# Sums and differences of x on Pool, and S1 as 64x64 TensorE tiles between S2 and S3

## The chip, the cores and the metric

The kernel runs on one core of one Trainium2 chip. The metric is the device time of one execution in microseconds (us), as the median of the fast runs. The engines are named as the profile names them: PE is TensorE's matmul and PEld its weight load, DVE is VectorE, ACT is ScalarE, POOL is GpSimd, SP is SyncE, which here only issues transfers. L377 is line 377 of that version of the kernel; the lines move a little from version to version. The code and diffs below are shortened; ... marks a cut inside a line or between lines.

Ratios below are the mean time of one kernel's runs over that of the other's runs of the same rounds on the same chip, so they are not quite the ratios of the medians that are quoted beside them.

## The reference

```python
X = np.fft.rfft(x, axis=1)                     # x: 8 x 3072 x 256, fp32
y = np.fft.irfft(X * (filt_r + 1j*filt_i), n=3072, axis=1)
t = y.reshape(24576, 256)
g = np.maximum(t @ w1, t @ w2)                 # w1, w2: 256 x 1024
out = g @ w_out                                # 1024 x 256
```

A long convolution by way of the Fourier transform is followed by a two-way maximum network on each of the 24,576 tokens.

## The kernel before

The transform of length 3072 = 128 x 24 is done with matmuls in four stages. S1 is a real transform of length 128 (table `C1`) for each of 24 columns. S2 is the 24-long transform with its twiddles (`U`), in 32 groups `t`. The filter is a multiplication on DVE. S3 goes back (`VP`, `VQ`), and S4 is the last transform of length 128 (`G1`). Between S1 and S2, and between S3 and S4, the data makes a round trip through HBM (`ad` to `bt`, `zd` to `zr`), which transposes it. The network is computed as relu(y(w1 - w2)) w_out + y(w2 w_out): `ph` is the first matmul, `gt` its relu, `po` the sum of both parts, `ot` the output tile of 512 tokens.

Batch 0 is done in a startup of about 49 us. From there on each tile of 512 tokens is 8 "steps". A step is one `ph` pair and one half of a `po`, about 1 us. A plan in the program hangs the transform's pieces for later batches onto step numbers. The program fixes the order of every engine's instructions.

```python
xpool = tile_pool(name="xpool", bufs=8)
apool = tile_pool(name="apool", bufs=5)          # at
pqpool = tile_pool(name="pqpool", bufs=6)
...
ps = tile_pool(name="ps", bufs=6, space=PSUM)    # px, pa, pz, ph, py share six banks
pso = tile_pool(name="pso", bufs=2, space=PSUM)  # po
opool = tile_pool(name="opool", bufs=2)          # ot: two output buffers

def load_x(b, c):                                # Pool issues it; fp32 becomes bf16 on the way
    t_ = xpool.tile([128, 4, D], BF16)
    G.dma_start(out=t_, in_=x[b].rearrange("(p n) d -> p n d", n=24)[:, 4*c:4*c+4, :])

def f1(b, c, E=None):                            # S1: one 128x128 matmul, 512 columns
    pa = ps.tile([128, 2, D], FP32)
    TE.matmul(pa, C1, xb[b, c // 2][:, 2*(c % 2):2*(c % 2)+2])
    evac(E or S, at[:, ...], pa)                 # ACT copies, SP writes at to HBM
    if c % 2 == 1: nc.sync.dma_start(out=ad[b][...], in_=at)

def f1_read(b):                                  # four transfers, SP
    bt[b] = bpool.tile([128, 32, D], BF16); ...

def gen_f2(b):                                   # eight groups per batch
    for g in (4, 5, 6, 7, 2, 3, 1, 0):
        px = two banks; eight matmuls px <- bt, U           # S2, 64x64 tiles
        pq = DVE: px * F                                    # two of 1.2 us
        S3 of the group before: pz = two banks; 16 matmuls; ACT copies pz to zt; SP writes zt
        yield

def moe_o(tt, j):                                # second half of the network
    ...
    if j % 4 == 3: V.tensor_copy(ot[tt][...], po[tt])       # DVE
    if j == 7:     G.dma_start(out=..., in_=ot[tt])         # Pool issues the output transfer

plan_x(n, ...)  -> load_x at given steps;  plan_f1(n, ...) -> f1 x 12, then f1_read
plan_f2(n, ...) -> nine calls of the group generator, then z_read
```

Of the kernel before, what the change touches and what calls it, by code (L numbers as in the profile page):

```python
# [8 lines left out]
FP32 = mybir.dt.float32  # L9
BF16 = mybir.dt.bfloat16  # L10
AF = mybir.ActivationFunctionType
OP = mybir.AluOpType

B = 8
# [15 lines left out]
def kernel(  # L30
# [38 lines left out]
    I128 = const.tile([128, 128], BF16)  # L69

    dram = ctx.enter_context(tc.tile_pool(name="dram", bufs=2, space=bass.MemoryType.DRAM))
    xpool = ctx.enter_context(tc.tile_pool(name="xpool", bufs=8))
    apool = ctx.enter_context(tc.tile_pool(name="apool", bufs=5))
    bpool = ctx.enter_context(tc.tile_pool(name="bpool", bufs=2))
    pqpool = ctx.enter_context(tc.tile_pool(name="pqpool", bufs=6))
    zpool = ctx.enter_context(tc.tile_pool(name="zpool", bufs=2))
    zrpool = ctx.enter_context(tc.tile_pool(name="zrpool", bufs=2))
    late = ctx.enter_context(tc.tile_pool(name="late", bufs=1))
    w2b = late.tile([128, 2, HID], BF16)
    w2T = late.tile([128, 8, D], BF16)  # L80
    setup = ExitStack()
    ps = None
    init = setup.enter_context(tc.tile_pool(name="init", bufs=1))
# [4 lines left out]
    def bank2(shape, dtype, name, tag=None):  # L88
        if tag is None:
            ring.append(ring.pop(0))  # L90
            tag = ring[-1]
        return p2.tile(shape, dtype, tag=tag, name=name)
# [63 lines left out]
    def patch_f0():  # L156
        nc.sync.dma_start(out=F0[12:13, 1, 0], in_=filt_i[1536:1537, :])
        nc.sync.dma_start(out=F0[12:13, 0, 0], in_=filt_r[1536:1537, :])
# [45 lines left out]
    load_f(1)  # L204

    Ct = init.tile([128, 128], BF16)

    def table_c():
        V.memset(kc[:, :, 1, 0:1], 32.0)
        V.memset(kc[:, 1, 0, 0:1], 64.0)  # L210
        p128 = init.tile([128, 1], FP32)
        V.tensor_scalar(p128, pid, 1.0 / 128.0, None, OP.mult)
        uc = init.tile([128, 2, 2, T], FP32)
        rc = init.tile([128, 2, 2, T], FP32)
        V.tensor_scalar(uc[:, 0], kc[:, 0], p128, 0.25, OP.mult, OP.add)
        V.tensor_scalar(uc[:, 1], kc[:, 1], p128, 0.5, OP.mult, OP.add)
        V.tensor_scalar(uc[:, 1, 0, 0:1], kc[:, 1, 0, 0:1], p128, 0.25, OP.mult, OP.add)
        V.tensor_scalar(rc, uc, RND, RND, OP.add, OP.subtract)
        V.tensor_tensor(uc, uc, rc, OP.subtract)
        for a in range(2):  # L220
            for b in range(2):
                S.activation(Ct.rearrange("p (b a h c u) -> p a b c h u", b=2, a=2, h=4, c=2)[:, a, b],
                             uc[:, a, b].rearrange("p (c h u) -> p c h u", c=2, h=4), AF.Sin, bias=zero, scale=TWO_PI)
        Cv = C1.rearrange("p (h c u b a) -> p a b c h u", h=4, c=2, b=2, a=2)
        for a in range(2):
            for b in range(2):
                S.activation(Cv[:, a, b], uc[:, a, b].rearrange("p (c h u) -> p c h u", c=2, h=4),
                             AF.Sin, bias=zero, scale=TWO_PI)
# [56 lines left out]
    def table_e(t1):  # L285
        V.tensor_scalar(t1, pid, 12.0, None, OP.is_equal)
        V.tensor_scalar(e0[:, 0:1], pid, 0.0, t1, OP.is_equal, OP.add)
        V.tensor_scalar(e0[:, 1:2], e0[:, 0:1], -1.0, 1.0, OP.mult, OP.add)
        V.tensor_scalar(e0[:, 0:1], e0[:, 0:1], -0.5, 1.0, OP.mult, OP.add)
        V.memset(F0[:, :, :, 0:1], 0.0)  # L290

    def sines_u(q):
        Uv = U.rearrange("p t (r x) -> p t r x", r=2)
# [13 lines left out]
        G.tensor_copy(F[0:64, :, 1, 0], F0[:, :, 1])  # L307

    def tables_pe():
        pv = bank2([128, 16, 2, 64], BF16, "pv")  # L310
        for u in range(16):
            TE.transpose(pv[:, u], U[:, 2 * u:2 * u + 2].rearrange("p c x -> p (c x)"), I128)
        V.tensor_copy(VP[:, :, :, 0:48], pv[:, :, :, 0:48])

    def table_g():
        pg = p2.tile([128, 128], BF16, tag="px", name="pg", bufs=4)
        TE.transpose(pg, C1, I128)
        S.activation(G1, pg, AF.Copy)

    def tables_q(h, E):  # L320
# [49 lines left out]
    def f1(b, c, E=None):  # L370
# [8 lines left out]
        if c % 2 == 1:  # L379
            nc.sync.dma_start(out=ad[b][:, 2 * c - 2:2 * c + 2], in_=at)  # L380

    def f1_read(b):
        bt[b] = bpool.tile([128, T, D], BF16, tag="bt", name="bt")
        src = ad[b].rearrange("(t b a) n d -> b (a n) t d", b=2, a=2)
        for h in (1, 0):
            for blk in range(2):
                nc.sync.dma_start(out=bt[b][64 * blk:64 * blk + 48, 16 * h:16 * h + 16],  # L387
                                  in_=src[blk][:, 16 * h:16 * h + 16])


    def z_read(b, h):
# [5 lines left out]
    def gen_f2(b):  # L397
        bt_ = bt[b]
        zd[b] = dram.tile([T, 96, D], BF16, tag="zd", name="zd")
        pend = []  # L400
        zt = None

        def s3(g, pq):
            nonlocal zt
            if zt is None:
                zt = zpool.tile([128, 2, 4, D], BF16, tag="zt", name="zt")
                made.clear()
            pz = [ps.tile([128, 2, D], FP32, tag="ps", name="pz") for _ in range(2)]
            for i in range(2):
                for ri, W in enumerate((VP, VQ)):  # L410
                    for c, k in QUADS:
                        TE.matmul(pz[c][64 * k:64 * k + 64, i], W[64 * c:64 * c + 56, 2 * g + i, k],  # L412
                                  pq[k][64 * c:64 * c + 56, ri, i], start=(ri == 0), stop=(ri == 1))
            o = 2 * (g % 2)
            for c in range(2):
                S.activation(zt[0:ROWS, c, o:o + 2], pz[c][0:ROWS], AF.Copy)  # L416
            made.append(g)
            if len(made) == 2:
                t0 = 8 * (g // 2)
                for k in range(2):  # L420
                    nc.sync.dma_start(out=zd[b][t0:t0 + 8, 48 * k:48 * k + 48].rearrange("t p d -> p t d"),
                                      in_=zt[64 * k:64 * k + 48].rearrange("p c u d -> p (c u) d"))
                zt = None

        made = []
        for g in (4, 5, 6, 7, 2, 3, 1, 0):
            px = [ps.tile([128, 2, D], FP32, tag="ps", name="px") for _ in range(2)]
            for i in range(2):
                for k, c in QUADS:
                    t_ = 8 * (g // 2) + 4 * c + 2 * (g % 2) + i  # L430
                    TE.matmul(px[k][64 * c:64 * c + 64, i], U[64 * k:64 * k + 48, 4 * g + 2 * i + c],  # L431
                              bt_[64 * k:64 * k + 48, t_], start=True, stop=True)
            pq = []
            for k in range(2):
                pq.append(pqpool.tile([128, 2, 2, D], BF16, tag="pq", name="pq"))
                V.tensor_tensor(pq[k][0:FROWS],  # L436
                                px[k][0:FROWS].rearrange("p (o i) d -> p o i d", o=1).to_broadcast([FROWS, 2, 2, D]),
                                F[0:FROWS, :, k, 2 * g:2 * g + 2], OP.mult)
            pend.append((g, pq))
            if len(pend) > 1:  # L440
                s3(*pend.pop(0))
            yield
        while pend:
            s3(*pend.pop(0))
        yield
# [152 lines left out]
            pass  # L598

    table_c()  # L600
    Zt = late.tile([128, 2, 128, N2], BF16, name="Zt")
    At = init.tile([128, 4, 64, T], BF16, name="At")
    zeros(At[:, :, 48:64].rearrange("p h m t -> p h (m t)"), [4, 512])
    zeros(U.rearrange("p t (q x) -> p (t q) x", q=2)[:, :, 24:32], [64, 8])
# [17 lines left out]
    sines_u(1)  # L622
    first_s1(2, S)
    expand_f(5, 0, V)
    sines_u(2)
    first_s1(3, S)
    expand_f(0, 0, V)
    first_s1(4, V, 2)
    first_s1(5, S, 2)
    expand_f(6, 0, V)  # L630
    expand_f(1, 1, S, 2)
    table_e(t1)
    load_f0()
    patch_f0()
    first_t1(1, V)
    first_t1(2, V)
    expand_f(7, 0, S)
    pend = []
    for n, g in enumerate(order):
        pend.append(first_s2(g, n in (0, 1, 2, 4, 6)))  # L640
# [40 lines left out]
    def plan(step, fn, *a):  # L681
        todo.setdefault(step, []).append((fn, a))

    def plan_x(n, steps):
        for c, s_ in enumerate(steps):
            plan(s_, load_x, n, c)

    def plan_f1(n, steps, read):
        for c, s_ in enumerate(steps):
            plan(s_, f1, n, c)  # L690
        plan(read, f1_read, n)

    def plan_f2(n, steps, z1, z0):
        g = []
# [11 lines left out]
    def spaced(first, gap, count):  # L706
        return [first + int(gap * i) for i in range(count)]
# [4 lines left out]
        plan(int(0.6 * (c - 1)), f1, 1, c, (S, V)[c % 2])  # L712
    plan(6, f1_read, 1)
    plan_f2(1, spaced(17, 1.9, 9), 28, 34)
    plan_x(2, spaced(8, 4, 6))
    plan_f1(2, spaced(34, 1, 12), 46)
    plan_f2(2, spaced(60, 2.5, 9), 74, 81)
    plan_x(3, spaced(44, 4, 6))
    plan_f1(3, spaced(70, 1.5, 12), 88)
    plan_f2(3, spaced(104, 3, 9), 121, 129)  # L720
    plan_x(4, spaced(90, 4, 6))
    plan_f1(4, spaced(112, 1.8, 12), 132)
    plan_f2(4, spaced(151, 3.3, 9), 169, 179)
    for n in range(5, B):
        o = 48 * (n - 5)
        plan_x(n, spaced(138 + o, 4, 6))
        plan_f1(n, spaced(158 + o, 1.9, 12), 180 + o)
        plan_f2(n, spaced(197 + o, 3.4, 9), 216 + o, 226 + o)

    def in_f2(step):  # L730
# [44 lines left out]
```

## Time and profile before

| | before |
|---|---|
| time, median of 2 runs | 532.39 us (532.07 to 532.71) |
| profiled span | 529.9 us |
| TensorE's mean granted clock | 0.998 |

The first fence holds lines of the profile's page. The first line is the busy time of each engine. The next lines cut the span into 40 slices: the busy share of PE and of Pool in tenths, the clock granted to TensorE, and the busy share of the 16 DMA engines.

```profile
PE 509.2 (96%) x5133; PEld 346.6 (65%) x5212; DVE 321.9 (61%) x436; ACT 336.0 (63%) x597; POOL 77.5 (15%) x130
...
PE   8898999999999999999999999999999999999994
...
POOL 6684011111001200011001200021000000000000
PEclk9999999999999999999999999999999999999999
DMA  7993687877678947599468956699377826521122
```

After the first tenth PE is busy nearly always, at full clock. Pool is nearly idle. The DMA engines are not: several slices are at 9.

The timeline shows how long an S1 matmul and a group hold PE (columns: start, duration, engine, line, operation, output and inputs, shapes, count).

```profile
250.69 0.38 PE L377 MATMUL pa<-xb,C 128*128 128x512 bf16 x1
...
250.91 0.59 PE L558 MATMUL ph<-y__4122,Wd 128*128 128x512 bf16 x2
...
251.98 0.41 PE L431 MATMUL px<-bt,U 48*64 48x256 bf16 x8
...
252.22 0.28 PE L412 MATMUL pz<-pq,VP 56*64 56x256 bf16 x4
...
252.22 0.12 PEld L412 LDWEIGHTS <-VQ 56*64 56x64 bf16 x4
252.33 0.28 PE L412 MATMUL pz<-pq,VQ 56*64 56x256 bf16 x4
```

A matmul's duration includes its way through the pipeline, so the time that it holds PE is read from the next start: 0.22 us from pa to ph. Eight px tiles take 0.24 us and four pz tiles 0.11 us. A 128x128 matmul of 512 columns takes 0.22 us, so 256 columns take half of that, and these are the times of four tiles running side by side.

The list of waits (who waited for whom; total us, times, longest) shows how little slack there is on PE.

```profile
PE ph L558 <- DVE pq L436: 2.3, 7, 0.3
...
PE pz L412 <- DVE pq L436: 0.8, 1, 0.8
...
DVE ot L585 <- DMA out_dram<-ot: 2.7, 1, 2.7
```

In the groups of Pool's instructions there is one operation like the new fold:

```profile
L339 POOL TENSOR_TENSOR Wd<-wf 128x1024 bf16<-128x1024 f32 x2 | 4.7, 2358 | 0.0
```

The page's DMA part gives the two queues that matter: packets, MB, and the share of 16 engines' span. q1 carries what SP issues, q0 what Pool issues. The last line is the x transfer before the change: its count, its size, and the median time from issue to landing in us.

```profile
q1 hardware_dynamic: 52196, 44.84, 37.2%
q0 software_dynamic: 16208, 41.95, 30.6%
...
xb<-in_x_dram POOLq DMA_DIRECT2D x48, 256.0 KB, 8.1
```

### The profile page before, as it was taken

How to read it: one execution, taken by the hardware profiler on the slowest of the kernel's cores; microseconds unless marked ns; L12 is line 12 of the kernel's file. 1: busy time of each engine (PE TensorE's matmuls, PEld its weight loads, DVE VectorE, ACT ScalarE, POOL GpSimd, SP SyncE). 2: the span in 40 equal slices, each digit the busy share in tenths (PEclk: the TensorE clock that was granted, in tenths of full speed). 3: DMA queues.
4: the chain of work that ended last, by engine and by line, in shares of the span. 5: the costliest groups of instructions: out<-in, count | busy, mean ns of one | idle time of the engine just before them, and what ended most of it. 6: DMA issues, size and time to landing. Idle time of an engine off the chain costs nothing.

```text
span 529.9 us, 12176 instructions
## 1 busy us (share of the span) xinstructions
PE 509.2 (96%) x5133; PEld 346.6 (65%) x5212; DVE 321.9 (61%) x436; ACT 336.0 (63%) x597; POOL 77.5 (15%) x130
## 2 busy tenths in 40 slices
PE   8898999999999999999999999999999999999994
PEld 3556656666667666676667666676667666677774
DVE  8886579245854576348763677438763688443431
ACT  6786657856785588746775577655775566555540
POOL 6684011111001200011001200021000000000000
PEclk9999999999999999999999999999999999999999
DMA  7993687877678947599468956699377826521122
GB/s 145 285 189 62 162 167 174 228 215 170 170 207 222 218 132 213 144 197 208 143 212 164 261 134 175 186 191 224 112 203 207 146 94 160 130 80 79 42 81 79
DMA packets 68459, 87.57 MB, mean 165 GB/s; under 512 B 4082, under 2 KB 48756, under 8 KB 67412
## 3 DMA queue, kind: packets, MB, share of 16 engines
q1 hardware_dynamic: 52196, 44.84, 37.2%
q0 software_dynamic: 16208, 41.95, 30.6%
q8 instruction: 40, 0.66, 0.5%
q14 instruction: 15, 0.12, 0.1%
HBM read 54.79 MB, written 47.19 MB: 192 GB/s over the span
## 4 chain that ended last, share of the span: by engine, by line
PE 72%; DMA 3%; DVE 1%; issue 1%; ACT 0%; SPq 0%
PE po L583 28%; PE ph L558 24%; PE po L578 7%; PE pz L412 4%; PE px L431 3%; PE py L542 3%; PE pa L377 3%; DMA bt<-ad 2%; DVE pq L436 1%; DMA ad<-at 1%; DVE ot L585 0%; ACT y__5598 L545 0%; SPq L387 0%
## 5 line engine op out<-in xcount | busy, mean ns | idle before, releaser
L563 ACT ACTIVATE gt<-ph 128x512 bf16<-128x512 f32 x308 | 182.3, 599 | 109.4 <-PE ph L558 108.2
L583 PE MATMUL po<-Wo,gt 128*128 128x256 bf16 x1536 | 229.8, 273 | 3.0
L583 PEld LDWEIGHTS <-gt 128*128 128x128 bf16 x1536 | 150.3, 98 | 57.5
L436 DVE TENSOR_TENSOR pq<-px,F 120x1024 bf16<-120x1024 f32 x112 | 131.7, 1218 | 28.0 <-PE px L431 27.5
L585 DVE COPY ot<-po 128x512 f32<-128x512 f32 x96 | 66.2, 689 | 111.2 <-PE po L583 108.2
L558 PEld LDWEIGHTS <-Wd 128*128 128x128 bf16 x768 | 70.1, 98 | 27.8 <-issue 12.5
L590 POOL DMA_DIRECT2D out_dram<-ot x47 | 25.2, 537 | 430.8 <-DVE ot L585 409.5
L416 ACT ACTIVATE zt<-pz 112x512 bf16<-112x512 f32 x112 | 60.7, 594 | 43.1 <-PE pz L412 37.9
L561 DVE TENSOR_SCALAR gt<-ph 128x512 bf16<-128x512 f32 x76 | 52.1, 686 | 29.6 <-PE ph L558 22.5
L476 ACT ACTIVATE at<-pa 128x512 bf16<-128x512 f32 x78 | 46.8, 600 | 12.4 <-PE pa L377 10.7
L377 PE MATMUL pa<-xb,C 128*128 128x512 bf16 x83 | 31.1, 381 | 0.1
L542 PE MATMUL py<-G,zr 128*128 128x128 bf16 x384 | 29.4, 219 | 0.7 <-ACT zr L476 0.7
L412 PE MATMUL pz<-pq,VP 56*64 56x256 bf16 x448 | 28.5, 271 | 0.8 <-DVE pq L436 0.8
L412 PE MATMUL pz<-pq,VQ 56*64 56x256 bf16 x448 | 27.9, 268 | 0.0
L542 PEld LDWEIGHTS <-zr 128*128 128x128 bf16 x384 | 24.8, 98 | 3.7 <-issue 1.9
L101 POOL DMA_DIRECT2D xb<-in_x_dram x48 | 26.2, 556 | 1.5 <-DMA Fs<-in_filt_i_dram 1.3
L431 PE MATMUL px<-bt,U 48*64 48x256 bf16 x448 | 23.4, 281 | 0.1
L431 PEld LDWEIGHTS <-U 48*64 48x64 bf16 x448 | 8.2, 104 | 12.1 <-issue 11.8
L492 DVE TENSOR_TENSOR pq<-px,F 120x1024 bf16<-120x1024 f32 x11 | 13.2, 1221 | 3.8 <-PE px L483 1.3
L412 PEld LDWEIGHTS <-VP 56*64 56x64 bf16 x448 | 13.1, 106 | 2.7 <-issue 1.5
L476 ACT ACTIVATE F<-pf 128x1024 bf16<-128x1024 f32 x10 | 10.3, 1026 | 6.2 <-PE pf L134 5.8
L412 PEld LDWEIGHTS <-VQ 56*64 56x64 bf16 x448 | 13.2, 107 | 0.0
(383 smaller groups left out, 580.4 us busy)
## 6 DMA issues: line engine op xcount, KB each, us to landing
out_dram<-ot POOLq DMA_DIRECT2D x47, 512.0 KB, 4.5
xb<-in_x_dram POOLq DMA_DIRECT2D x48, 256.0 KB, 8.1
ad<-at SPq DMA_DIRECT2D x42, 256.0 KB
bt<-ad SPq DMA_DIRECT2D x28, 384.0 KB
zd<-zt SPq DMA_DIRECT2D x56, 192.0 KB
zr<-zd SPq DMA_DIRECT2D x14, 768.0 KB
wf<-in_moe_w_dram POOLq DMA_DIRECT2D x2, 1024.0 KB, 9.8
Fs<-in_filt_r_dram POOLq DMA_DIRECT2D x1, 768.0 KB, 7.0
```

The costliest lines, as they stand in the source:

```text
L377: TE.matmul(pa, C1, xb[b, c // 2][:, 2 * (c % 2):2 * (c % 2) + 2], start=True, stop=True)
L412: TE.matmul(pz[c][64 * k:64 * k + 64, i], W[64 * c:64 * c + 56, 2 * g + i, k], pq[k][64 * c:64 * c + 56, ri, i], start=(ri == 0), stop=(ri ...
L416: S.activation(zt[0:ROWS, c, o:o + 2], pz[c][0:ROWS], AF.Copy)
L431: TE.matmul(px[k][64 * c:64 * c + 64, i], U[64 * k:64 * k + 48, 4 * g + 2 * i + c], bt_[64 * k:64 * k + 48, t_], start=True, stop=True)
L436: V.tensor_tensor(pq[k][0:FROWS], px[k][0:FROWS].rearrange("p (o i) d -> p o i d", o=1).to_broadcast([FROWS, 2, 2, D]), F[0:FROWS, :, k, 2 ...
L476: S.activation(out_, in_, AF.Copy)
L542: TE.matmul(py[:, n], zr[b][:, 4 * i + n, 128 * dc:128 * dc + 128], G1, start=True, stop=True)
L558: TE.matmul(ph, Wd[:, dc, 128 * j:128 * j + 128], y_[:, dc].rearrange("p a b -> p (a b)"), start=(dc == 0), stop=(dc == 1))
L561: V.tensor_scalar(gt[tt][:, j], ph, 0.0, None, OP.max)
L563: S.activation(gt[tt][:, j], ph, AF.Relu)
L583: TE.matmul(p_, g_[:, jj, 128 * n:128 * n + 128], Wo[:, jj], start=False, stop=(jj == 7))
L585: V.tensor_copy(ot[tt][:, n - 1:n + 1], po[tt])
```

## The change

A transform of length 128 splits into two of half the contraction: even frequencies need x[p] + x[p+64], odd ones x[p] - x[p+64]. So for batches 2 to 7 x is loaded as fp32 with both rows side by side, Pool forms sum and difference in bf16, and S1 becomes four 64x64 tiles of 512 columns in place of two 128x128 matmuls. The four can run side by side, so S1 should take half of PE's time. S2 and S3 are 64x64 tiles already, so the S1 tiles of the next batch are put inside the groups, between px and pz, and need no change of tile mode.

```diff
+    def load_p(b, c):                     # SP issues it, fp32 stays fp32
+        if c == 0: big[b] = late.tile([128, 3, 2, 2 * D], FP32, tag="l0", name="xf")
+        xb[b, c] = big[b][:, c] if c < 3 else late.tile([128, 2, 2 * D], FP32, tag="l%d" % (c - 2))
+        for m in range(2):
+            nc.sync.dma_start(out=xb[b, c][64 * m:64 * m + 64], in_=...)
+    def fold_x(b, c):                     # Pool
+        xf = xb[b, c]
+        xb[b, c] = xpool.tile([128, 2, 2 * D], BF16, tag="xb", name="xd")
+        for i, op in enumerate((OP.add, OP.subtract)):
+            G.tensor_tensor(xb[b, c][:, i], xf[:, 0], xf[:, 1], op)
+    def f1_half(b, c):
+        ...
+        at = apool.tile([128, 4, D], BF16, tag="at", name="at")
+        pa = [ps.tile([128, 2, D], FP32, tag="ps", name="pa") for _ in range(2)]
+        for m, i in QUADS:
+            TE.matmul(pa[m][64*i:64*i+64], C1[64*m:64*m+64, 64*i:64*i+64], xb[b, c][64*m:64*m+64, i], ...)
+        for m in range(2): S.activation(at[:, 2*m:2*m+2], pa[m], AF.Copy)
+        nc.sync.dma_start(out=ad[b][:, 4*c:4*c+4], in_=at)
     # f1_read: eight transfers in place of four
     # gen_f2, in each group, after pq and before S3 of the group before:
+            if b + 1 < B and j in (0, 1, 3, 4, 6, 7):
+                f1_half(b + 1, (0, 1, 3, 4, 6, 7).index(j))
     def plan_x(n, steps):
         for c, s_ in enumerate(steps):
-            plan(s_, load_x, n, c)
+            plan(s_, load_p, n, c)
+            plan(s_ + 5, fold_x, n, c)
-    plan_f1(3, spaced(70, 1.5, 12), 88)
+    plan(83, f1_read, 3)
-    plan_x(4, spaced(90, 4, 6))
+    plan_x(4, spaced(76, 3.5, 6))
     ... (the other batches alike; small moves in the startup; xpool 8 -> 7 buffers; tables reordered)
```

## The prediction

> **What bounds the kernel now.** TensorE. The page gives PE 96% of the 529.9 us span, DVE 61%, ACT 63%, POOL 15%. The table by stretches shows PE busy 19.5 to 19.9 of every 20 us from 120 to 500 us at full clock. The list of waits holds only about 3.6 us in which PE sat before ph or pz. From the first ph matmul (49 us) on, a microsecond added to or taken from PE's in-order queue is a microsecond of time.
>
> **What the change removes.** In the timeline an S1 matmul (pa, 128x128, 512 columns) holds PE 0.22 us (250.69, next start 250.91). Twelve per batch, six batches: 15.5 us. Folding halves contraction and outputs, so six groups of four 64x64 matmuls replace twelve. The S2/S3 tiles show that four run together: eight px matmuls of 256 columns take 0.24 us, four pz 0.11 us. (The Trainium skill, "TensorEngine Tiling (Array Packing)", Key Properties, says so; this trace agrees.) So 36 x 0.22 = 7.9 us should leave PE. No mode switch is added: the tiles stand between S2 and S3 of the same mode.
>
> **What it adds off PE.** 72 Pool folds, estimated at 1.2 us each from Pool's 128x1024 subtraction (2.36 us): 85 us, on an engine 85% idle. x arrives as fp32 from the SP queue, some 20 steps before use. F1 reads are twice the issues, same bytes. I expect these hidden.
>
> **What it moves, and the catch.** Six PSUM banks serve px, pa, pz, ph, py. A group with S1 now takes px, px, pa, pa, pz, pz in one burst: all six. The built order with its bank assignment shows that in about 26 of 36 groups the next ph takes the bank of the first pa. From the trace: group start to pa end 0.47 us, 0.2 until ACT starts, 0.6 to copy, 0.05 to release: 1.3 us; ph could start at 1.0. PE stalls 0.3 us, 26 times: 8 us. Four pz follow a pa in its bank directly (0.8 us each); py or ph after pa or px add a few us. Counted so, the kernel before has 3.2 us of such stalls (its trace agrees), the kernel after about 17. S1 of batch 2 also moves from free MoE steps into the tightest groups (spacing 1.9 steps), where ACT's work (estimate 28 us) exceeds PE's (26 us). ("PSUM Bottleneck" in that page: tiling speeds up TensorE, not PSUM evacuation.) The wait of px for bt in batch 5 (about 0.45 us) should go: S1 ends earlier.
>
> **Sum.** 532.4 - 7.9 + 14 - 1 = 538 if every counted stall is real; 525 if none is. Startup: perhaps 1 us. I predict **534 us**, range **526 to 542**; faster by over 2%: 0.04, within 2%: 0.88, slower by over 2%: 0.08.
>
> **What would show each step.** Four pa tiles take about 0.22 us. In the list of waits PE ph waits for ACT at (the pa copy), about 0.3 us each, over 20 times: new. Pool busy rises to about 140 us; pq stays 1.22 us. MoE stretches without groups stay 8.25 us per tile of 512 tokens; the period of a batch (60.0 us now) changes by under 1 us.
>
> **What would make it wrong.** ACT copying sooner than counted, so that the stalls vanish (toward 525); x or folds arriving late, PE then waiting for Pool; folds delaying output transfers; four 512-column tiles not overlapping fully.

## The result, and the profile after

| | before | after |
|---|---|---|
| time, median of 2 runs | 532.39 us | 582.9 us (581.5 to 584.31) |
| ratio | 1 | 1.095 (95%: 1.083 to 1.107) |
| profiled span | 529.9 us | 579.7 us |
| mean granted clock | 0.998 | 0.962 |
| DMA bytes | 87.57 MB | 97.03 MB |

Executions over 1.5% slower than the fastest of the same kernel are left out of the means. The change makes the kernel 9.5% slower, and the result lies far outside the predicted range. The page's lines after:

```profile
PE 520.9 (90%) x5206; PEld 352.9 (61%) x5284; DVE 322.5 (56%) x437; ACT 337.2 (58%) x597; POOL 147.9 (26%) x168
...
PE   8898859995999969995999996999789999999997
...
POOL 6681163126004070232405240051400000000000
PEclk9999979998799989998999997999979999999999
DMA  8982995898368954989449983789535873451102
```

PE's row has holes of 5 to 7, one in each batch's period, and the clock falls to 7 or 8 in the same slice or the next. Pool's row shows where the folds stand: near the holes. The list of waits says who waited:

```profile
POOL xd L402 <- DMA xf<-in_x_dram: 102.3, 12, 17.4
...
DVE ot L622 <- DMA out_dram<-ot: 49.7, 6, 11.1
...
PE pa L410 <- DVE pq L471: 15.2, 5, 6.4
...
PE pa L410 <- POOL xd L402: 7.0, 2, 6.4
...
PE pa L410 <- DVE y__4127 L584: 5.9, 1, 5.9
PE ph L595 <- ACT at L413: 5.3, 21, 0.3
PE pz L447 <- DVE pq L471: 4.9, 2, 4.2
PE pz L447 <- ACT at L413: 2.1, 4, 0.7
```

Waits of PE for a pq or y of VectorE are in the list, up to 6.4 us each. The new bank waits, the ones that the prediction counted, are there too, with 5.3 us. But the first two lines are far larger: Pool waited 102 us for x, and VectorE 50 us for an output buffer, where it was 2.7 us before. One of the six long PE waits, read from the timeline by engine (SP's and Pool's queue first, then VectorE and PE), shows how these are connected:

```profile
183.13 8.83 SPq L423 DMA_DIRECT2D bt<-ad  x8
192.00 8.52 SPq L395 DMA_DIRECT2D xf<-in_x_dram  x8
...
202.32 4.94 POOL L402 TENSOR_TENSOR xd<-xf 128x512 bf16<-128x512 f32 x4 [17.36 <-DMA xf<-in_x_dram]
207.22 0.56 POOL L627 DMA_DIRECT2D out_dram<-ot  x1
...
211.97 0.69 DVE L622 COPY ot<-po 128x512 f32<-128x512 f32 x1 [8.35 <-DMA out_dram<-ot]
212.58 2.35 DVE L471 TENSOR_TENSOR pq<-px,F 120x1024 bf16<-120x1024 f32 x2
...
209.24 0.41 PE L466 MATMUL px<-bt,U 48*64 48x256 bf16 x8
213.85 0.42 PE L447 MATMUL pz<-pq,VP 56*64 56x256 bf16 x1 [4.20 <-DVE pq L471]
```

Read it from the top. SP issues eight bt transfers in 8.8 us and only then the remaining x, two transfers for each of four tiles. Pool works in the program's order and stands at a fold for 17.36 us until x lands. The output transfer of a finished tile stands behind the folds of two x tiles in the same queue, so it is issued only at 207.22. Both ot buffers are full by then, so VectorE's next copy into ot waits for 8.35 us. VectorE's next instruction, pq, starts only at the end of that copy, at 212.58, and PE, whose next matmuls need this pq, waits for it. The six PE waits of this length are 6.38, 6.35, 4.20, 5.92, 3.53 and 3.84 us, 30.2 us in all. The first, at 78 us, is PE waiting for batch 2's fold directly. At each of the other five VectorE stood at an ot copy (8.35 to 11.1 us) just before.

The table by stretches (columns: stretch, its length, busy time of PE, PEld, DVE, ACT and POOL, granted clock, DMA share, GB/s) gives the second cost, the clock after the wait:

```profile
209.00:215.00 6.00, 1.09 (x16) 0.32 (x15) 3.03 (x4) 0.40 (x1) 4.25 (x5) 0.81 0.36 144
215.00:221.00 6.00, 5.95 (x47) 3.49 (x51) 3.48 (x4) 2.77 (x5) 0.54 (x1) 0.62 0.42 124
```

The Trainium skill, "TensorE: Matmul & The Clock Gate", HAM oscillation, says that a PE pause longer than its window of about 3.4 us halves the clock. This trace agrees: after the pause of 4.20 us the clock from 215 to 221 us is 0.62 although PE is busy again. The same view, taken behind each of the six pauses for about six microseconds, gives 0.50 to 0.62.

On PE as a whole, the waits of the list from 49 us on add up to 44.9 us, where they were 4.0 us before.

The groups of the two new operations themselves:

```profile
L402 POOL TENSOR_TENSOR xd<-xf 128x512 bf16<-128x512 f32 x72 | 89.3, 1264 | 141.9 <-DMA xf<-in_x_dram 102.3
...
L410 PE MATMUL pa<-xd,C 64*64 64x512 bf16 x144 | 17.5, 405 | 28.1 <-DVE pq L471 15.2 <-POOL xd L402 7.0 <-DVE y__4127 L584 5.9
```

A fold takes 1264 ns. The S1 tiles take what they should: in the timeline four of them hold PE from 204.65 to 204.87, 0.22 us. The two DMA queues after:

```profile
q1 hardware_dynamic: 63012, 63.72, 49.6%
q0 software_dynamic: 11024, 32.51, 17.9%
```

As share times span the two queues took (37.2% + 30.6%) of 529.9 us = 359 us of all 16 engines before, and (49.6% + 17.9%) of 579.7 us = 391 us after. The bytes written to the chip for x have doubled.

### The profile page after: what moved, and what is told of

It is laid out like the page before. It is cut to its first block, busy times and chain, and to the rows that moved or that the text cites. A ratio compares the mean times of both kernels' runs of the same rounds, so it can differ in the third digit from the quotient of the medians.

```text
span 579.7 us, 12530 instructions
## 1 busy us (share of the span) xinstructions
PE 520.9 (90%) x5206; PEld 352.9 (61%) x5284; DVE 322.5 (56%) x437; ACT 337.2 (58%) x597; POOL 147.9 (26%) x168
## 2 busy tenths in 40 slices
DMA packets 74093, 97.03 MB, mean 167 GB/s; under 512 B 5106, under 2 KB 49780, under 8 KB 73044
## 3 DMA queue, kind: packets, MB, share of 16 engines
q1 hardware_dynamic: 63012, 63.72, 49.6%
q0 software_dynamic: 11024, 32.51, 17.9%
## 4 chain that ended last, share of the span: by engine, by line
PE 62%; DMA 18%; ACT 5%; DVE 5%; SPq 4%; issue 3%; POOL 2%; POOLq 0%; DVEq 0%; ACTq 0%
PE po L620 22%; PE ph L595 20%; DMA xf<-in_x_dram 6%; DMA out_dram<-ot 5%; PE po L615 5%; SPq L423 3%; PE pz L447 3%; ACT at L413 3%; PE px L466 3%; DMA zd<-zt 2%; PE py L579 2%; POOL xd L402 2%; DVE pq L471 2%; DMA bt<-ad 2%; PE pa L410 2%
## 5 line engine op out<-in xcount | busy, mean ns | idle before, releaser
L620 PE MATMUL po<-Wo,gt 128*128 128x256 bf16 x1536 | 234.5, 277 | 4.0 <-issue 0.7
L620 PEld LDWEIGHTS <-gt 128*128 128x128 bf16 x1536 | 152.6, 99 | 61.1 <-issue 3.3
L471 DVE TENSOR_TENSOR pq<-px,F 120x1024 bf16<-120x1024 f32 x112 | 131.7, 1219 | 30.6 <-PE px L466 29.7
L402 POOL TENSOR_TENSOR xd<-xf 128x512 bf16<-128x512 f32 x72 | 89.3, 1264 | 141.9 <-DMA xf<-in_x_dram 102.3
L413 ACT ACTIVATE at<-pa 128x512 bf16<-128x512 f32 x72 | 39.1, 595 | 57.8 <-PE pa L410 57.8
L410 PE MATMUL pa<-xd,C 64*64 64x512 bf16 x144 | 17.5, 405 | 28.1 <-DVE pq L471 15.2
L447 PE MATMUL pz<-pq,VP 56*64 56x256 bf16 x448 | 31.7, 283 | 7.0 <-DVE pq L471 4.9
L447 PE MATMUL pz<-pq,VQ 56*64 56x256 bf16 x448 | 30.7, 281 | 0.0
L410 PEld LDWEIGHTS <-C 64*64 64x64 bf16 x144 | 5.0, 109 | 30.6 <-DVE pq L471 16.6
L447 PEld LDWEIGHTS <-VP 56*64 56x64 bf16 x448 | 15.6, 109 | 11.6 <-issue 6.8
L447 PEld LDWEIGHTS <-VQ 56*64 56x64 bf16 x448 | 14.7, 111 | 1.8
```

The lines of the kernel that those rows point to most:

```text
L402: G.tensor_tensor(xb[b, c][:, i], xf[:, 0], xf[:, 1], op)
L413: S.activation(at[:, 2 * m:2 * m + 2], pa[m], AF.Copy)
L447: TE.matmul(pz[c][64 * k:64 * k + 64, i], W[64 * c:64 * c + 56, 2 * g + i, k], pq[k][64 * c:64 * c + 56, ri, i], start=(ri == 0), stop=(ri ...
L471: V.tensor_tensor(pq[k][0:FROWS], px[k][0:FROWS].rearrange("p (o i) d -> p o i d", o=1).to_broadcast([FROWS, 2, 2, D]), F[0:FROWS, :, k, 2 ...
L620: TE.matmul(p_, g_[:, jj, 128 * n:128 * n + 128], Wo[:, jj], start=False, stop=(jj == 7))
```

## The experiments

Theory Q, formed from the trace: x comes late at the fold; the fold holds the output transfer behind it on Pool; the two output buffers run out; VectorE and then PE stop. Rival D: the fp32 bytes load the DMA engines beyond what they can do, wherever the instructions stand. Rival B: the new PSUM traffic and ACT's work in the groups cost the time, as the prediction had it, only more of it.

| run | what differs from the changed kernel | median us | ratio to before (95%) |
|---|---|---|---|
| e1_three_ot | three ot buffers | 542.35 | 1.019 (1.017 to 1.022) |
| e2_fold_later | folds 14 steps after the load, not 5 | 538.97 | 1.013 (1.011 to 1.015) |
| e3_x_on_pool | fp32 x issued by Pool | 560.49 | 1.056 (1.050 to 1.062) |
| e4_no_fold | no fold, result wrong | 545.27 | 1.025 (1.021 to 1.028) |
| e6_batch2_early | e2, and batch 2's x earlier | 530.81 | 0.998 (0.997 to 1.000) |
| e7_pa_first | e2, and S1 at the head of the group | 533.92 | 1.005 (1.002 to 1.007) |
| e8_both | e6 and e7 together | 524.89 | 0.987 (0.986 to 0.989) |
| e9_load_early | x loaded 12 steps earlier, folds in place | 538.72 | 1.013 (1.011 to 1.015) |
| e10_x_bf16 | e3, with x cast to bf16 on the way | 536.49 | 1.008 (1.006 to 1.010) |
| e11_fold_9 | folds 9 steps after the load | 551.63 | 1.037 (1.035 to 1.039) |
| e12_three_ot_again | e1 once more, for a profile | 543.98 | one run, state unknown |

The kernel before ran at 531.7, 531.7 and 532.3 us beside them on three chips: e1 to e4 on the first, e6 to e9 on the second, e10 to e12 on the third. All versions except e4 gave correct results.

### e1_three_ot and e12_three_ot_again: one more output buffer

```diff
-opool bufs=2, apool bufs=5, pqpool bufs=6
+opool bufs=3, apool bufs=4, pqpool bufs=5
```

The third buffer gets its room from two other pools, so the edit changes those as well.

> The changed kernel (582.9 us) with three output buffers ot instead of two (room from one at and one pq buffer less). Theory Q (queues): the time is lost because a fold on Pool waits for an x transfer that comes late, the output transfer issued from the same Pool queue waits behind it, the two ot buffers run out, VectorE stops in order and then TensorE. A third ot buffer gives about 8 us more slack, so five of the six long PE waits (3.5 to 6.4 us each, about 24 us, plus half-clock time after them) vanish or shrink below 1 us: 545 to 555 us; the wait of PE for the first fold (6.4 us near 78 us) stays. Rival D (bandwidth: fp32 x costs the DMA engines more and they are the limit): no more bytes move or less, the waits only move elsewhere: 575 us or more. Rival B (PSUM banks and ACT): 580 us.

> The version with three output buffers (fast runs 541.2 to 543.0 us), only to get a profile, since the one before fell in a run of 2584 us. Theory Q: VectorE's waits for output buffers near zero where they were 50 us, Pool's waits for x still near 100 us, PE's waits for the first folds of batch 2 still near 7 us.

Measured: 541.2 to 543.0 us in three runs, a little below the expected 545 to 555 us. The profiled execution of e1 was an outlier of 2584 us, in which even plain matmuls were several times longer; it is left out, and e12 took a profile again, at 543.98 us. VectorE's waits for output buffers are gone from its list. Pool waits for x as long as ever, and only PE's waits for batch 2's folds remain long (list of waits of e12):

```profile
PE pa L410 <- POOL xd L402: 7.0, 2, 6.3
...
POOL xd L402 <- DMA xf<-in_x_dram: 111.8, 16, 17.7
```

This is the step in the chain that rivals D and B cannot explain: with the same folds, the same bytes and the same order, one buffer more takes back 40 of the 50 us. Pool's idling does no harm by itself; it harms through the output buffers.

### e2_fold_later and e11_fold_9: the fold's place on Pool

```diff
-            plan(s_ + 5, fold_x, n, c)
+            plan(s_ + (5 if n == 2 else 14), fold_x, n, c)      # e2;  9 in place of 14 in e11
```

> The changed kernel with the folds of batches 3 to 7 placed 14 steps after their loads in Pool's order instead of 5 (batch 2 as it was). Nothing else moves. Theory Q: x has landed when Pool comes to the fold, so Pool no longer holds the output transfers: the list of waits loses most of Pool's 102 us for x and VectorE's 50 us for output buffers, and the time falls to 540 to 555 us. Rival D: x still lands as late, and PE now waits for folds instead: above 570 us. Rival B: 580 us.

> The changed kernel (582.9 us) with the folds of batches 3 to 7 placed 9 steps after their loads: a dose between 5 (582.9 us) and 14 (539.0 us). Theory Q: Pool waits for x until the same time, but the output transfers that stand before the moved folds go out; four steps are about 4 us, so the five PE waits that came through the output buffers (6.4, 4.2, 5.9, 3.5, 3.8 us) shrink by about 4 us each to a sum near 4 us: 543 to 555 us. If only the largest distance helps, the time stays above 570 us.

Measured: 538.97 us with 14 steps and 551.63 us with 9, beside 582.9 us with 5. The second is inside the expected range; the first is 1 us below the expected 540 to 555 us, so the change paid slightly more than theory Q had said. The list of waits of e2:

```profile
POOL xd L402 <- DMA xf<-in_x_dram: 66.4, 7, 17.1
...
PE pa L410 <- POOL xd L402: 7.3, 2, 6.7
PE ph L595 <- ACT at L413: 6.3, 25, 0.3
DVE ot L622 <- DMA out_dram<-ot: 2.3, 1, 2.3
```

The waits for output buffers are back at 2.3 us (49.7 us in the changed kernel), and the long PE waits of batches 3 to 7 are gone. One part of the expectation missed: Pool still waits 66 us for x. About 30 us of it are batch 2's folds, which were not moved and still hold PE for 7.3 us. The rest costs nothing that the lists show: VectorE hardly waits for an output buffer any more. In e11 the dose shows in between:

```profile
DVE ot L622 <- DMA out_dram<-ot: 12.2, 2, 7.7
```

The 44 us between 5 and 14 steps can be put together roughly. PE's waits for pa and for pq in S3 fall from 33.0 us (28.1 + 4.9) to 7.3 us. The clock makes up most of the rest: the mean granted clock goes from 0.962 to 0.990. As a share of the span missing from full clock that is 22 us against 5 us (an estimate; a part of it lies inside the waits).

### e9_load_early: the load's place instead of the fold's

```diff
-            plan(s_, load_p, n, c)
+            plan(s_ - (0 if n == 2 else 12), load_p, n, c)
```

> The changed kernel (582.9 us) with its folds where they were, and the x transfers of batches 3 to 7 issued 12 steps earlier, so that nearly all stand before the bt reads in the SP queue. It is the mirror of moving the folds: distance between transfer and fold 17 steps instead of 5. Theory Q (x late at the fold): Pool no longer waits, VectorE's 50 us of waits for output buffers go, 538 to 548 us. If it is the folds' place among Pool's instructions as such (their 89 us of work ahead of the output transfers), not the late x, the time stays above 570 us.

Measured: 538.72 us, as e2. The folds stand exactly where they stand in the changed kernel, with all of their 89 us of work, and VectorE's wait for output buffers is 2.8 us. So neither the folds' work nor their place among the output transfers costs the 44 us by itself. It is that x comes too late for the fold, whichever of the two is moved. (The earlier loads also stand ahead of the bt reads in SP's queue, so e9 by itself does not tell distance from order.) The list of waits of e9:

```profile
POOL xd L402 <- DMA xf<-in_x_dram: 30.2, 3, 17.0
```

These three waits are all before 81 us, at batch 2's folds, whose loads were not moved. For batches 3 to 7 no fold waits for x any more.

### e3_x_on_pool and e10_x_bf16: why x is late

```diff
-            nc.sync.dma_start(out=xb[b, c][64 * m:64 * m + 64],
+            G.dma_start(out=xb[b, c][64 * m:64 * m + 64],
     # e10 also: the xf tiles are BF16, so the transfer casts
```

> The changed kernel with the same fp32 x transfers issued from Pool instead of the SP queue, same bytes, same steps, folds as they were. Theory Q with the SP queue as the root: x no longer queues behind the eight bt transfers and the zr transfers, so it lands within 5 to 10 us of its step; Pool's waits for x fall below a third of 102 us, the long PE waits mostly go, 540 to 555 us. If x is late for lack of bandwidth (rival D), it stays late: 575 us or more. Rival B: 580 us.

> The version with x issued from Pool (560.5 us), x cast to bf16 on the way: half the bytes written on chip, everything else in the same place, folds 5 steps after the loads. If the doubled bytes of fp32 are what makes x late (rival D), x lands sooner and the time falls by 10 us or more, to 550 us or less. Theory Q says that distance and order decide, not bytes: within 6 us of 560.5 us.

Measured: 560.49 us for e3 and 536.49 us for e10. The first is above the expected range, and Pool's waits for x fell to 57 us and not below a third of 102. The second falsifies what theory Q said of bytes. Issuing the same fp32 from Pool, past the bt transfers in SP's queue, took back 22 us, and with half the bytes written on the chip another 24 us went (the two ran on different chips; their ratios to before, 1.056 and 1.008, say the same). From the list of waits of e3:

```profile
POOL xd L402 <- DMA xf<-in_x_dram: 57.3, 17, 7.2
DVE ot L622 <- DMA out_dram<-ot: 26.0, 6, 7.2
...
PE px L466 <- DMA bt<-ad: 9.7, 4, 4.7
```

and of VectorE's waits of e10:

```profile
DVE ot L622 <- DMA out_dram<-ot: 11.1, 4, 3.8
```

In e3 part of the chain through the output buffers remains (26.0 us). Besides, x and bt are now issued at the same time and seem to slow each other: PE waits 9.7 us for bt, where it was 1.0 us. This agrees with what the Trainium skill, "DMA: Bandwidth & Descriptors", Issuing engines are not separate DMA queues, says: transfers issued by different engines end up on the same 16 DMA engines. So two things act on x. It stands behind bt in SP's queue, and the DMA engines are heavily loaded in those stretches: in the changed kernel the table by stretches gives a DMA share of 1.09 from 183 to 200 us. A share above 1 means that packet times overlap in it, so it shows load and not a limit reached; the rate was 197 GB/s there and 261 GB/s in the next nine microseconds. Pool's waits for x are 102 us in the changed kernel, 57 us with x issued by Pool, and 44.5 us with half the bytes as well. Rival D is right about a part of the lateness. It is wrong that the bytes cost the time wherever the instructions stand: e2 and e9 move the same 97.03 MB and lose 7 us, not 50. How much of the lateness belongs to each reason alone was not separated: e10 also makes each pair of folds 0.2 us shorter, and x as bf16 over SP was not run.

### e4_no_fold: the tiles alone

```diff
 load: straight to bf16 into the tile that S1 reads, issued by Pool
-fold_x: two operations on Pool
+fold_x: nothing                              # wrong result, on purpose
```

> Wrong on purpose: x is loaded by Pool straight to bf16 into the tile that S1 reads, in the same rows, half of it dropped in effect, and nothing is folded. S1 tiles stay inside the groups. It measures the tiles and their PSUM traffic alone. The prediction's count (7.9 us of S1 saved, about 9 us of new bank waits) gives 530 to 536 us; if the bank waits had been counted too high, 525 us. Theory Q: no PE wait above 1 us is left. Rival B would keep it above 560 us.

Measured: 545.27 us, above the expectation, with no fold at all. The expectation that no wait of PE above 1 us would be left missed as well. From its list of waits:

```profile
PE py L571 <- DMA zr<-zd: 8.4, 3, 3.4
PE ph L587 <- ACT at L405: 6.3, 25, 0.3
```

The bank waits are near the count, and Pool holds nothing. But PE waits 8.4 us for zr and 3.6 us for bt. In this plan x, zr and bt are asked for in the same steps. When x is not held up in SP's queue, it seems to take the engines' time from the other two. That reading was not tested by itself. Less these 12 us the time would be 533 us, inside the expected range of 530 to 536 us (an estimate; what the waits cost in clock is not counted).

### e6_batch2_early, e7_pa_first and e8_both: taking the rest back

```diff
 # e6, on top of e2: batch 2's first three tiles use the small buffers, which are free early
-    plan_x(2, (5, 7, 8, 10, 11, 13))
+    plan_x(2, (0, 0, 1, 8, 9, 10))               # folds at steps 10, 11, 13, 19, 21, 23
 # e7, on top of e2: in each group
-            px ...; pq ...; f1_half(b + 1, ...); S3
+            f1_half(b + 1, ...); px ...; pq ...; S3
```

> The version with later folds (539.0 us), and batch 2's first three x tiles loaded at steps 0 and 1, ahead of the first bt read, its last three just after it, its folds at steps 10 to 22. Theory Q: the last long wait of PE for a fold (6.7 us and 0.6 us near 78 us) goes, with the clock that it cost after it: 529 to 532 us, no PE wait over 1 us left. If that wait was only filling time that PE would have lost in another way: 537 us or more.

> The version with later folds (539.0 us), and the S1 tiles at the head of a group, before px, instead of between px and pz. Counted with the trace's durations, the copy of the first pa then ends at about the time when the next ph could start: the 25 waits of PE ph for ACT at (6.3 us in all) shrink below 2 us, and the time falls by 4 to 6 us to 533 to 535 us. If those waits are slack that PE loses anyway, the time stays at 538 to 539 us.

> Later folds, batch 2 early and S1 first in the group together. If the three losses are independent and add, 523 to 527 us, 1 to 1.7% under the kernel before, which is the gain of 7.9 us that the tiles were meant to bring. If the change has another cost that has not been named, 530 us or more.

(The fold steps in the expectation of e6 are given as 10 to 22; as built the last one is at 23.)

Measured: 530.81, 533.92 and 524.89 us, all within the ranges. In e6 PE no longer waits for a fold. In e7 the 25 waits of ph for the pa copy are gone from PE's list: the copy starts one S2 earlier, and its end meets the next ph. The Trainium skill, "TensorEngine Tiling (Array Packing)", PSUM Bottleneck, warns that tiling does not speed up the emptying of PSUM; here the cost of that was a matter of order, and went away without any more copying power. The ratio to before falls by 0.015 from e2 to e6, by 0.009 from e2 to e7, and by 0.026 to e8, so within the intervals the two gains add up. In e6 the waits of PE from 49 us on add up to 11.5 us, and in e8 to 4.1 us, as in the kernel before (4.0 us). In e8 Pool waits about as long for x as in e2:

```profile
POOL xd L402 <- DMA xf<-in_x_dram: 68.4, 9, 11.1
```

Yet e8 is 1.3% faster than the kernel before. The gain is 6.8 us of the 7.9 us that the tiles were meant to bring.

## Why the prediction was wrong

- **The kernel before is bound by PE's in-order queue: right.** In e6 PE's waits are 7.5 us longer than before, the tiles take 7.9 us less, and the time is the same within 1 us. In e8 the waits are as before, and the time is 6.8 us shorter.
- **S1 tiles hold PE 0.22 us for four, 7.9 us saved: right.** The tiles take 0.22 us, and e8 reaches 6.8 us under before.
- **The bank waits: right in kind, about twice too large in the sum.** For ph about 0.3 us, 26 times, or 8 us, was predicted; measured were 5.3 us in 21 waits of at most 0.3 us, and in e2 6.3 us in 25. The four pz behind a pa took 2.1 us where 3.2 us was counted. In all the sum allowed 14 us for new stalls, and in e6, where the folds hold nothing, PE's waits grew by 7.5 us. E7 removes the ph waits.
- **The folds' own cost: right.** 1264 ns measured, 1.2 us estimated; Pool's busy time 147.9 us, predicted about 140. DVE's pq stays at 1219 ns beside it. The Trainium skill, "GPSIMD Engine Reference", Key points, expects contention only with VectorE instructions in a two-port mode or with two on-chip (SBUF) inputs; pq has one input in PSUM, and this trace agrees.
- **"I expect these hidden": this is the step that failed.** It was argued from Pool being 85% idle and x being loaded "some 20 steps before use". The first number was right; by the plan the second is 27 to 35 steps for batches 3 to 7 and 12 to 17 for batch 2. Both were the wrong ones to look at. The use that matters for the queues is not S1's but the fold's, 5 steps later. And the question was not how much Pool works but what stands behind an instruction that waits. Behind the fold stood the output transfer, with two buffers of slack, and behind those VectorE and PE. Measured were 102 us of Pool waiting for x, 50 us of VectorE waiting for an output buffer, and the long PE waits of 30.2 us with the slow clock behind them; folds 9 steps later take 44 us off the time. With this step mended, and nothing else but batch 2's loads and folds, e6 takes 530.81 us, which is inside the predicted range. The prediction named this among the things that could make it wrong ("folds delaying output transfers"), but gave it no number and no place in the range. The number could have been had from the profile before: in the page, an x transfer issued by Pool took a median of 8.1 us to land, against 5 steps of about 1 us. That x then landed still later, up to 17.4 us after Pool had begun to wait, could not be read from there.
- **The clock was missed.** Behind the five waits on VectorE and the one on a fold (3.53 to 6.38 us) the clock was 0.50 to 0.62 for about six microseconds; the mean clock fell from 0.998 to 0.962.
- **The smaller points.** A tile of 512 tokens without groups takes 8.3 us in both kernels, and the first ph starts at 49.0 and 48.9 us, so neither the network's stretches nor the startup matter. The period of a batch was to change by under 1 us and went from 60.0 to 67.7 us (batch 3 to 4). The small relief forecast for bt in batch 5 was not tested by itself; the changed kernel's only waits of px for bt, 1.0 us, are at batch 1's first groups.
- **Twice as many bt transfers, "same bytes": true, but not free.** The eight of them occupy SP's queue for 8.8 us in the stretch shown (the four of the kernel before took 3.3 to 7.0 us), and x waits behind them. No run had the new kernel with four.

The 50 us are therefore: about 44 us from the distance between load and fold in batches 3 to 7 (e2, e9), 8 us from the same distance in batch 2 (e6), 5 us from the bank waits (e7), less the gain of the tiles. What stays open is how x's lateness divides between SP's order and the DMA engines' load, and why zr comes late in e4. The parts are differences of total times, with the clock in them.

## What to carry to other kernels

An idle engine is not free to take work if its queue also issues transfers: an instruction that waits for data holds everything behind it, so count the distance from the load to the first instruction that waits for it, and the slack (buffers) of whatever stands behind that. Break such a chain at the cheapest link: here one number in the plan took back 44 us and needed no memory, an output buffer more 40 us, and x issued by Pool at half the bytes 46 us. When tiles enter a burst that uses all PSUM banks, try those whose bank is needed first at the head of the burst; this was tried here with one kind of tile, S1.

## What the Trainium skill lacked or had wrong

- "GPSIMD Engine Reference" describes Pool's compute and its part in issuing transfers, but not that a waiting compute instruction holds the issue of later transfers. Here one fold waited 17.36 us at the head of Pool's queue, the output transfer behind it was issued only after it, and moving the folds by 9 steps was worth 44 us. "Perfetto Trace Analysis", Tensor Engine Instruction, does say that GPSIMD is strictly in order, which agrees.
- "GPSIMD Engine Reference", Elementwise, gives 4497 ns for an fp32 add of 2048 elements, which would scale to 1124 ns for 512 (an estimate from the page's figure). The fold of 512 elements with bf16 output took 1264 ns, the 1024-element subtraction 2358 ns, and the fold of e10 with bf16 input 1152 ns (median). The page has no figure for these.
- "TensorEngine Tiling (Array Packing)", PSUM Bottleneck, advises more copying engines; it lacks the advice on order. Putting S1 at the head of the group took away 25 waits of 6.3 us in all, with the same copies.
- "TensorE: Matmul & The Clock Gate" was right: the pause of 4.20 us was followed by a granted clock of 0.62. Its warning that clock records cannot always be trusted may bear on one execution of e1, whose cause stays open: it took 2584 us, the po matmuls had a mean of 930 ns in place of 277, and the recorded clock was 1.0.
- No page was found that says what fp32 instead of bf16 on the on-chip side costs a transfer from HBM. With folds that are 0.2 us shorter per pair as the only other difference, it was here the difference between 560.5 and 536.5 us, with the same bytes read from HBM.
